# Strassen's scheme for the second product of a token mixer, with the mixer cut into thirds

## The chip, the cores and the metric

The kernel runs on one core of one Trainium2 chip. The metric is the device time of one execution in microseconds (us). Each version was run several times; quoted times are medians of the fast runs. A profile is one execution of its own, so its span differs a little from the median.

## The reference, cut to what matters

```python
# attention (recurrent, gated): B=4 batches, H=8 heads, S=768 tokens, D=48
state = f[:, :, t, :, None] * state + np.einsum('bhd,bhe->bhde', k[:, :, t], v[:, :, t])
y[:, :, t] = np.einsum('bhd,bhde->bhe', q[:, :, t], state)
# mixer, on x = y as (4, 768, 384):
xt = x.transpose(0, 2, 1)
h = xt @ U @ V                       # rank 32, over tokens
u = x + h.transpose(0, 2, 1)
ch = np.maximum(u @ w_ch1, 0.0) @ w_ch2   # 384 -> 1536 -> 384
out = u + ch
```

Everything is float32. "First product" is `u @ w_ch1`, "second product" is the one by `w_ch2`.

## The kernel before

Attention works on 16 units (a batch and a pair of heads each). Each unit is prepared on VectorE, ScalarE and GpSimd while TensorE (PE) works on an earlier one. The mixer of a batch comes as a list of pieces that are put between the attention pieces of the next batch; for the last batch nothing is left to put them between. The builder then orders each engine's instructions by itself, and each engine runs its own list in that order.

The mixer's two products, in halves of 384 tokens:

```python
def ch1(a, i):
    pm = ps_mm.tile([P, 512], F32, name="pz", tag="mm")      # ps_mm has 2 buffers
    for m in range(NDC):
        nc.tensor.matmul(pm[:, 0:HALF], lhsT=w1[:, m, i * P : (i + 1) * P], rhs=uT[a][:, m, :],
                         start=(m == 0), stop=(m == NDC - 1))
    z[a, i] = zp.tile([P, HALF], F32, name="z")
    nc.scalar.activation(z[a, i], pm[:, 0:HALF], AF.Relu)

def ch2(a, s):
    t = a * TPH + s
    pm = ps_mm.tile([P, 512], F32, name="po", tag="mm")
    for i in range(NFC):                                      # 12
        nc.tensor.matmul(pm[:, 0:DM], lhsT=z[a, i][:, s * P : (s + 1) * P], rhs=w2[:, i, :],
                         start=(i == 0), stop=(i == NFC - 1))
    o = three.tile([P, DM], F32, name="o")
    nc.vector.tensor_tensor(o, x[:, t, :], pm[:, 0:DM], ALU.add)
    nc.sync.dma_start(out=out[b, t * P : (t + 1) * P, :], in_=o)
```

The preparation of a unit in batches 2 and 3 (units 8 to 15), cut:

```python
def gates():
    fT = one.tile([P, S], F32, name="fT")                # the pool "one" has one buffer a name
    turned(fT, r["f"])                                   # VectorE, 32x32 transposes
    nc.scalar.activation(by_chunk[:, :, 1:C], fv[:, :, 1:C], AF.Sigmoid)   # into fz[n % 2]
    ...
def keep():   X = one.tile(...); nc.vector.tensor_tensor_scan(X backwards, fz, ends ...)  # shortened
def keys():   turned(kT, r["k"]); nc.gpsimd.tensor_tensor(kT, kT, X, ALU.mult)
def read():   Y = one.tile(...); nc.vector.tensor_tensor_scan(Y, fz, starts ...)          # shortened
def queries(): turned(qT, r["q"]); nc.gpsimd.tensor_tensor(qT, qT, Y, ALU.mult)
```

## Time and profile before

| | before |
|---|---|
| time, median (range of 4 runs) | 589.89 us (589.7 to 591.07) |
| PE busy / VectorE / ScalarE / GpSimd | 550.6 / 244.8 / 121.8 / 62.4 us |
| first matmul of the second product (po) | at 115.0 us |
| last stage (mixer of batch 3 alone) | from 490.2 to 583.4 us |

The engine line of the page gives busy time and share of the span. In a group's row stand the line and engine, the output tile and its inputs, the shapes and the count, then busy time and the mean of one, then the idle time just before and what ended it. The chain of waits goes back from the last instruction to whatever released each step. The prediction shows these for the kernel before.

### The profile page before, as it was taken

The numbers are of one execution on the slowest core, as the hardware profiler recorded it, in microseconds if no ns is written. First come the engines' busy times: TensorE is split into PE (matmuls) and PEld (weight loads), VectorE is DVE, ScalarE is ACT, GpSimd is POOL, SyncE is SP. The second block draws the span as 40 slices with busy tenths as digits, with TensorE's granted clock in tenths as the row PEclk, the third lists the DMA queues.
The fourth block names the chain that finished last, engine by engine and source line by source line (L and its number), as shares of the span: only waits on it lengthen the run. The fifth ranks groups of instructions, "written<-read, shape, count | busy, mean of one in ns | idle before, by whom it ended". The sixth has DMA issues, their size and how long they took to land.

```text
span 589.1 us, 8824 instructions
## 1 busy us (share of the span) xinstructions
PE 550.6 (93%) x3737; PEld 344.2 (58%) x3737; DVE 244.8 (42%) x367; ACT 121.8 (21%) x260; POOL 62.4 (11%) x59
## 2 busy tenths in 40 slices
PE   5798897799989999989969999999999999999996
PEld 4687553457656556646645556566566555555553
DVE  5768769826697340638361620254211020000000
ACT  2233346502322103210112102120022003201200
POOL 2111125500022000113020200022000000000000
PEclk9557799999999999989998999999999999999998
DMA  9699827614652135133340310010000000000000
GB/s 167 145 225 177 189 59 208 150 35 104 164 128 54 43 83 132 42 79 94 100 107 0 87 41 13 1 21 14 28 1 1 15 13 14 1 13 27 2 14 31
DMA packets 75295, 41.56 MB, mean 71 GB/s; under 512 B 65774, under 2 KB 68846, under 8 KB 75246
## 3 DMA queue, kind: packets, MB, share of 16 engines
q1 hardware_dynamic: 75246, 40.91, 29.7%
q8 instruction: 31, 0.51, 0.4%
q14 instruction: 18, 0.15, 0.1%
HBM read 36.18 MB, written 4.72 MB: 69 GB/s over the span
## 4 chain that ended last, share of the span: by engine, by line
PE 80%; DVE 11%; DMA 3%; SPq 2%; ACT 1%; issue 1%; POOL 0%; DVEq 0%; ACTq 0%; POOLq 0%
PE po L158 32%; PE pz L149 26%; PE sc L404 5%; PE y L467 4%; PE pu L133 3%; PE pt L326 3%; DVE w_y L62 2%; DMA w_raw<-in_moe_V_dram 2%; PE y L458 2%; PE ds L430 2%; PE put L142 2%; DVE w_y L63 1%; SPq L232 1%; DVE X L358 1%; DVE Y L375 1%
## 5 line engine op out<-in xcount | busy, mean ns | idle before, releaser
L149 PE MATMUL pz<-uT,w 128*128 128x384 f32 x576 | 199.2, 497 | 13.1 <-ACT z L152 12.6
L158 PE MATMUL po<-w,z 128*128 128x384 f32 x576 | 192.2, 492 | 3.7 <-ACT z L152 3.7
L149 PEld LDWEIGHTS pz<-uT,w 128*128 128x128 f32 x576 | 106.3, 191 | 85.7 <-ACT z L152 12.9
L158 PEld LDWEIGHTS po<-w,z 128*128 128x128 f32 x576 | 109.0, 191 | 80.6 <-issue 5.9
L161 DVE TENSOR_TENSOR o<-x,po 128x384 f32<-128x384 f32 x24 | 13.3, 555 | 204.7 <-PE po L158 204.7
L152 ACT ACTIVATE z<-pz 128x384 f32<-128x384 f32 x96 | 46.8, 489 | 167.0 <-PE pz L149 167.0
L410 DVE TENSOR_TENSOR A<-sc,causal 128x768 f32<-128x768 f32 x32 | 30.3, 947 | 63.2 <-PE sc L404 63.2
L358 DVE TENSOR_TENSOR_SCAN X<-fz,ends 128x768 f32<-128x768 f32 x16 | 28.1, 1755 | 33.1 <-ACT fz L347 23.9
L341 POOL TENSOR_TENSOR kT<-kT,X 128x768 f32<-128x768 f32 x8 | 14.6, 1820 | 243.4 <-DVE kT L307 243.4
L404 PE MATMUL sc<-qT,kT 48*128 48x128 f32 x384 | 38.9, 312 | 0.2 <-DVE kT L338 0.2
L404 PEld LDWEIGHTS sc<-qT,kT 48*128 48x128 f32 x384 | 29.6, 204 | 14.2 <-issue 11.2
L467 PE MATMUL y<-v_nat,A 128*64 128x48 f32 x768 | 31.0, 245 | 0.0
L64 POOL TENSOR_TENSOR w<-w_y,w_r 128x384 int32<-128x384 int32 x24 | 23.9, 995 | 65.1 <-DVE w_y L63 65.1
L375 DVE TENSOR_TENSOR_SCAN Y<-fz,starts 128x768 f32<-128x768 f32 x16 | 28.1, 1756 | 5.8 <-POOL qT L341 5.2
L467 PEld LDWEIGHTS y<-v_nat,A 128*64 128x64 f32 x768 | 28.5, 159 | 1.7 <-issue 0.3
L473 ACT COPY x<-y 128x576 f32<-128x576 f32 x16 | 10.2, 636 | 61.2 <-PE y L467 61.2
L458 PE MATMUL y<-st,qT 48*64 48x48 f32 x640 | 18.0, 242 | 5.0 <-DVE st L441 3.6
L144 ACT COPY uT<-put 128x384 f32<-128x384 f32 x24 | 10.7, 480 | 53.7 <-PE put L142 53.7
L458 PEld LDWEIGHTS y<-st,qT 48*64 48x64 f32 x640 | 13.9, 149 | 13.0 <-issue 5.0
L62 DVE TENSOR_SCALAR w_y<-w_y 128x384 uint32<-128x384 uint32 (+1 forms) x27 | 20.3, 752 | 0.7
L133 PE MATMUL pu<-h,V 128*128 128x384 f32 x48 | 19.4, 514 | 0.8 <-DVE x L134 0.8
L341 POOL TENSOR_TENSOR qT<-qT,Y 128x768 f32<-128x768 f32 x8 | 17.2, 2156 | 17.8 <-DVE X L365 11.7
(61 smaller groups left out, 338.0 us busy)
## 6 DMA issues: line engine op xcount, KB each, us to landing
w_raw<-in_moe_w_ch_dram SPq DMA_DIRECT2D x24, 384.0 KB, 3.7
v_nat<-in_v_dram SPq DMA_DIRECT2D x32, 144.0 KB, 2.8
out_dram<-o SPq DMA_DIRECT2D x24, 192.0 KB, 1.9
f_raw<-in_f_logit_dram SPq DMA_DIRECT2D x31, 142.0 KB, 3.1
k_raw<-in_k_dram SPq DMA_DIRECT2D x31, 142.0 KB, 3.4
q_raw<-in_q_dram SPq DMA_DIRECT2D x31, 142.0 KB, 3.3
f_raw<-in_f_logit_dram SPq DMA_DIRECT2D x16, 144.0 KB, 4.9
k_raw<-in_k_dram SPq DMA_DIRECT2D x16, 144.0 KB, 5.0
```

The lines of the kernel that those rows point to most:

```text
L62: nc.vector.tensor_scalar(y, y, 3, 0x3FFFFFFF, ALU.logical_shift_left, ALU.bitwise_and)
L133: nc.tensor.matmul(pm[:, 0:DM], lhsT=V[:, t * P : (t + 1) * P], rhs=h[0], start=True, stop=True)
L149: nc.tensor.matmul(pm[:, 0:HALF], lhsT=w1[:, m, i * P : (i + 1) * P], rhs=uT[a][:, m, :], start=(m == 0), stop=(m == NDC - 1))
L152: nc.scalar.activation(z[a, i], pm[:, 0:HALF], AF.Relu)
L158: nc.tensor.matmul(pm[:, 0:DM], lhsT=z[a, i][:, s * P : (s + 1) * P], rhs=w2[:, i, :], start=(i == 0), stop=(i == NFC - 1))
L341: nc.gpsimd.tensor_tensor(t, t, T[of], ALU.mult)
L358: nc.vector.tensor_tensor_scan(backwards(X, S - 1, S), backwards(f, S, S), backwards(ends, S - 1, S), 0.0, ALU.mult, ALU.add,)
L375: nc.vector.tensor_tensor_scan(Y, f[:, 0:S], starts, 0.0, ALU.mult, ALU.add)
L404: nc.tensor.matmul(sc[:, par, c * C : (c + 1) * C], lhsT=T["k"][rows[par], chunk[g * G + c]], rhs=T["q"][rows[par], chunk[g * G + c]], sta ...
L410: nc.vector.tensor_tensor(T["A"][:, :, g * G : (g + 1) * G, :], sc[:, :, 0 : G * C].rearrange("p h (c i) -> p h c i", i=C), causal.unsquee ...
L458: nc.tensor.matmul(o(a, par, c), lhsT=T["q"][rows[par], c * C + a * HC : c * C + (a + 1) * HC], rhs=T["st"][rows[par], c - 1, :], start=(c ...
L467: nc.tensor.matmul(o(a, par, c), lhsT=T["A"][:, par, c, halves[a]], rhs=vt[:, c, par, :], start=False, stop=True, skip_group_check=True,)
```

## The change

Its intent: the second product of batches 1 to 3 takes 7 products of half size in place of 8, so PE streams an eighth less there. For this the mixer works on pairs of token blocks (thirds of 256 tokens), z and w2 are added and subtracted in quarters on VectorE, and the results are put together from PSUM. To make room, the gate tile fT shares the one buffer of Y.

```diff
+        def ch1(a, j):                       # two 128-row pieces of w1, 256 tokens: one PSUM bank
+            for i in range(2):
+                for m in range(NDC):
+                    nc.tensor.matmul(pm[:, i * 2 * P : (i + 1) * 2 * P], lhsT=w1[...], rhs=uT[a][:, m, :], ...)
+            nc.scalar.activation(z[a, c][:, k : k + 2, :]..., pm, AF.Relu)
...
+        def sums_of(a):                      # VectorE, 128x768 each, in the buffers of w_raw
+            add(S[1], part(a, 1, 0), part(a, 1, 1), ALU.add)
+            add(S[2], S[1], part(a, 0, 0), ALU.subtract)
+            add(S[3], part(a, 0, 0), part(a, 1, 0), ALU.subtract)
+            add(S[4], part(a, 0, 1), S[2], ALU.subtract)
...
+        def seven(a, step):                  # step 0 of 4; the others alike, tile name pw
+            if step == 0:
+                pm = products(a, (part(a, 0, 0), w2[:, 0:NI, lo]), (S[2], sums[2]))
+                nc.scalar.copy(s[:, hi], pm[:, lo])
+                add(s[:, lo], x0[:, lo], pm[:, lo], ALU.add)
+                add(s[:, hi], s[:, hi], pm[:, hi], ALU.add)
...
+        for a in range(NA - 1):
+            ahead = first(a + 1)
+            self.main += ready(a) + ahead[: NI // 2] + second(a) + ahead[NI // 2 :]
+        self.main += ready(NA - 1)
+        self.after = second(NA - 1)
...
-            fT = one.tile([P, S], F32, name="fT")
+            fT = one.tile([P, S], F32, name="fT", tag="Y")
...
-            Y = T["Y"] = one.tile([P, S], F32, name="Y")
+            Y = T["Y"] = one.tile([P, S], F32, name="Y", tag="Y")
...
+            if b == 1:
+                after.append((1, last_sum))  # w2's upper right quarter becomes a sum, in place
```

## The prediction

> **What bounds the kernel now.** I read the page's engine line first, then the groups, the chain of waits in order of time, the timeline around the holes that the chain shows, and the windows view for the clock. The engine line and groups:
>
> ```profile
> PE 550.6 (93%) x3737; PEld 344.2 (58%) x3737; DVE 244.8 (42%) x367; ACT 121.8 (21%) x260; POOL 62.4 (11%) x59
> L149 PE MATMUL pz<-uT,w 128*128 128x384 f32 x576 | 199.2, 497 | 13.1 <-ACT z L152 12.6
> L158 PE MATMUL po<-w,z 128*128 128x384 f32 x576 | 192.2, 492 | 3.7 <-ACT z L152 3.7
> L410 DVE TENSOR_TENSOR A<-sc,causal 128x768 f32<-128x768 f32 x32 | 30.3, 947 | 63.2 <-PE sc L404 63.2
> ```
>
> PE is the bound: 93% busy, and the two mixer products are 391 of its 551 us. VectorE has 42%, and so looks like a place with room. The 497 ns of one matmul is latency; the rate is in the chain, in whose last stage nothing but PE works:
>
> ```profile
> 490.22 23.49 PE pz L149 x72
> 513.71 23.22 PE po L158 x72
> 536.92 23.22 PE pz L149 x72
> 560.14 23.23 PE po L158 x72
> ```
>
> 23.22 us by 72 is 322.5 ns for one instruction of 384 columns. Until about 113 us the start is bound by loading and converting weights on VectorE: about 1.95 us for each of the twelve pieces of w2, back to back. From 114.96 us (first po) to 583.4 us PE is the chain but for a few holes. In the starts of matmuls I find three of over 1.5 us: 1.8 us at 174, 2.0 at 255, 4.9 at 304. The timeline at the largest:
>
> ```profile
> 302.58 1.81 POOL L341 TENSOR_TENSOR qT<-qT,Y 128x768 f32<-128x768 f32 x1 [3.91 <-DVE X L365]
> 304.42 1.76 DVE L375 TENSOR_TENSOR_SCAN Y<-fz,starts 128x768 f32<-128x768 f32 x1 [1.73 <-POOL qT L341]
> 306.09 2.06 DVE L307 STREAM_TRANSPOSE fT<-f_raw 128x768 f32<-128x768 f32 x1
> 308.19 0.84 ACT L353 ACTIVATE fz<-fT 128x762 f32<-128x762 f32 x1 [6.56 <-DVE fT L307]
> 308.93 0.47 ACT L152 ACTIVATE z<-pz 128x384 f32<-128x384 f32 x1
> 309.46 3.66 PE L149 MATMUL pz<-uT,w 128*128 128x384 f32 x6 [4.71 <-ACT z L152]
> ```
>
> This is the shape of all three. The eviction of pz takes 0.47 us, but stands in ScalarE's queue behind a sigmoid that waits for VectorE's transpose of the gates, which stands behind VectorE's queue, which waits for GpSimd. Both PSUM buffers of the mixer are full meanwhile, and PE stops. It costs twice, as the windows view shows after two of the holes, where the clock is half:
>
> ```profile
> 257.80:261.20 3.40, 3.40 (x7) 1.72 (x6) 0.00 (x0) 0.00 (x0) 0.00 (x0) 0.50 0.00 0
> 309.00:312.40 3.40, 2.94 (x5) 1.73 (x6) 0.00 (x0) 1.38 (x4) 0.00 (x0) 0.50 0.00 0
> ```
>
> Each half-clock window loses 1.7 us, so the holes and their windows come to 8.7 + 3.4 = about 12 us of 468.
>
> **What the Trainium skill says.** (1) "TensorE: Matmul & The Clock Gate", section "Wait — 56ns, not 53.3ns?": a warm matmul of N columns starts every N / 2.4 GHz + about 2.5 ns. The trace agrees if an f32 instruction streams its columns twice: 768 / 2.4 + 2.5 = 322.5 ns. (2) The same page, "LDWEIGHTS (loading the stationary operand)": 128 columns take 128 / 1.2 = 107 ns whatever the moving size, and are pulled ahead. The narrowest case here, the 128x128 transposes of x, start every 109 ns with a load each, so a load also hides behind 160 ns. (3) The same page, "The two states you'll see" under Part 1: an idle window of about 3.4 us halves the clock. The trace has the 3.4 us windows at half clock. (4) "GPSIMD Engine Reference", section 8: GpSimd shares its SBUF interfaces with VectorE instructions of two SBUF inputs. The trace agrees: a 128x6 TENSOR_SCALAR with a median of 172 ns took 1.60 us beside a GpSimd multiply that itself took 3.03 us in place of 1.82.
>
> **The change, part by part.**
>
> *Second product.* Before, batches 1 to 3 have 3 x 6 blocks x 12 = 216 f32 matmuls, 432 instructions of 322.5 ns = 139.3 us. After, 9 pairs x 7 products x 6 = 378 matmuls, 756 instructions of 192 columns, each 384 / 2.4 + 2.5 = 162.5 ns, = 122.9 us. Saved: 16.4 us.
>
> *First product.* 576 x 322.5 = 185.8 us become 864 instructions of 256 columns at 215.8 ns = 186.5 us: +0.7. So PE's stream shrinks by 15.7 us; 5.3 us of that lie in the last stage, where nothing can hide it.
>
> *VectorE.* A 128x768 addition is 0.95 us (the row of A), 384 columns 0.55 us (the row of o), so 192 about 0.35. For each pair: four sums of z, 3.8 us, and evictions of 3.4 us in place of 1.1. Nine pairs: +55 us, plus four sums of w2 at about 1.35 us: VectorE goes from 245 to about 305 us. That is still no bound on average. The first w2 sum stands in VectorE's queue amid the weight conversions that set the start of po: +1.4 us on the path.
>
> *Evictions of pz.* 96 of 384 columns become 72 of 512; each PSUM buffer lasts 2.6 us of PE in place of 1.9. It is a little easier on ScalarE.
>
> *The gate tile.* fT gets the one buffer of Y. Before, VectorE turned the gates far ahead (the last fT at 306 us, while the last kT comes at 404 us). Now fT of unit n+1 must wait until GpSimd has read Y of unit n. The built order of instructions shows it: in each unit of batches 2 and 3 VectorE now runs kT, qT, (wait for GpSimd), fT, (wait for the sigmoid), X, Y in one row, 2.1 + 2.1 + 1.9 + 2.1 + 0.9 + 1.8 + 2.2 = 13 us, with the new additions ahead of it or inside, and evictions that PE needs behind it.
>
> *Walking the new order by hand* with those durations, from the last matmul that VectorE waits for, I get these PE waits: around units 8 and 9 (end of batch 1) 2.3 us on state steps behind fT, then 6.4 us, since a state product needs a PSUM buffer whose eviction is behind Y of unit 9; 1.5 us in the first transition, where the in-place sum of w2 stands ahead of the additions to x; unit 11, 4.6 us (pz eviction behind the sigmoid); unit 12, 2.2; unit 13, 1.5; unit 14, 5.8 in three parts; unit 15, 2.0. Together 26.3 us, and two or three half-clock windows, 4.3 us: 30.6 in place of 12.1 and the 0.8 of the old transition, so +17.7 us. In the last stage the sums lie under three pieces of pz (7.8 us against 3.8), except for the last pair, where about 0.3 us show.
>
> *Sum:* 589.8 - 15.7 + 1.4 + 17.7 + 0.3 = 593.5 us. A walk like this takes every alignment at its worst, as PE's delay in one place gives VectorE a lead in the next. I take off a third of the added waits: about 588 us.
>
> **Rivals.** *A: the saving goes through.* The waits stay at the 12 us of before, and the time is 589.8 - 15.7 + 1.4 = about 575.5 us. For it: VectorE has a mean of 50% and preparations run a unit ahead of their use. Against it: the holes of before come from queue order, not from load, and the new order has more behind each sigmoid. *B: VectorE's row of preparation and sums takes the saving back,* as walked: 584 to 594 us. For it: the new order on VectorE and ScalarE, and the three holes of before of exactly this kind. *C: VectorE or GpSimd become slower by sharing SBUF,* as all 36 sums of z have two SBUF inputs and GpSimd multiplies beside them: another 1 us for each of some 16 multiplies, so up to 600 us and more. For it: the 1.60 and 3.03 us above; against it: only two cases before. *D: weight loads bound the narrow matmuls.* 756 loads of 190 ns (as recorded) in place of 162.5 would give back 20 us; the 109 ns transposes speak against it. DMA is no rival: its mean share is about a third or less after 233 us.
>
> **Range and chances.** B is the likeliest, and A and B overlap around 580. I put 588 us, with 80% in 574 to 600: the low end is A with hardly any slack, the high end B in full with part of C. Faster by over 2% means under 578 us, which needs nearly all of A: 0.22. Slower by over 2% means over 601.5 us: 0.08. Within: 0.70.
>
> **What would show it.** Right: pw instructions every 162.5 ns and pz every 215.8 in the last stage, which is then about 88 us in place of 93; VectorE busy about 305 us; the first po of batch 0 about 1.4 us later; more PE idle put down to ScalarE's z, to VectorE's o or w_y, and more half-clock stretches between 170 and 400 us than two. Wrong: PE holes of no more than 12 us in all in that stretch (then A, about 575 us), or pw at 190 ns (then D), or evictions at 512 columns that hold PE in the last stage.

## More of the kernel before

One more view is needed later: who waited for whom while the weights are loaded (82 to 115 us), with total, count and longest wait:

```profile
ACT w_y L59 <- POOL w L64: 10.0, 14, 0.9
PE pz L149 <- ACT z L152: 6.3, 4, 1.8
```

In this stretch ScalarE converts weights and also evicts pz; PE stands still 6.3 us for those evictions.

## The result and the profile after

| | before | after |
|---|---|---|
| time, median | 589.89 us | 584.25 us (583.41 to 585.78, 4 runs) |
| PE / VectorE busy | 550.6 / 244.8 us | 538.2 / 301.8 us |
| first po | 115.0 us | 110.8 us |
| first po to start of last stage | 375.3 us | 377.3 us |
| last stage | 93.2 us | 88.2 us |

The ratio is 0.9903, with a 95% interval of 0.9879 to 0.9928. Ratios here are the mean time of one kernel's fast runs over the mean of the other's of the same rounds, so they are not quite ratios of the medians. The change is faster by 1%, where PE's stream alone became 2.7% shorter.

Engines and groups of the page after:

```profile
PE 538.2 (93%) x4349; PEld 443.0 (76%) x4349; DVE 301.8 (52%) x461; ACT 121.5 (21%) x245; POOL 60.7 (10%) x59
L157 PE MATMUL pz<-uT,w 128*128 128x256 f32 x864 | 196.3, 384 | 3.5 <-ACT z L162 3.1
L194 PE MATMUL pw<-w,w_raw 128*128 128x192 f32 x432 | 76.4, 329 | 2.4 <-DVE w_raw L186 1.4
L194 PE MATMUL pw<-w,z 128*128 128x192 f32 x324 | 60.8, 339 | 8.9 <-DVE w_y L210 4.5
L407 DVE STREAM_TRANSPOSE fT<-f_raw 128x768 f32<-128x768 f32 x8 | 16.7, 2084 | 11.8 <-POOL qT L441 11.8
```

VectorE is at 302 us, as worked out. The last row is new: VectorE stands still 11.8 us for GpSimd before it may turn gates. The chain in the last stage gives the rates:

```profile
488.13 23.58 PE pz L157 x108
511.71 13.65 PE pw L194 x84
525.36 15.54 PE pz L157 x72
540.90 13.65 PE pw L194 x84
```

13.65 us by 84 is 162.5 ns, and 15.54 by 72 is 215.8 ns: PE streams without a pause, weight loads hidden. So the scheme delivers 5.0 of the 5.3 us that it promises where nothing else runs. In the middle the change delivers nothing: the stretch from the first po to the last stage is 2 us longer, though by the count of matmuls 10.4 us of stream are gone from it. The timeline at the first large hole, at the end of batch 1:

```profile
178.88 1.81 POOL L441 TENSOR_TENSOR qT<-qT,Y 128x768 f32<-128x768 f32 x1 [1.95 <-DVE Y L475]
180.72 2.08 DVE L407 STREAM_TRANSPOSE fT<-f_raw 128x768 f32<-128x768 f32 x1 [1.99 <-POOL qT L441]
182.90 0.84 ACT L453 ACTIVATE fz<-fT 128x762 f32<-128x762 f32 x1 [8.89 <-DVE fT L407]
183.76 1.76 DVE L458 TENSOR_TENSOR_SCAN X<-fz,ends 128x768 f32<-128x768 f32 x1 [0.96 <-ACT fz L453]
186.06 1.76 DVE L475 TENSOR_TENSOR_SCAN Y<-fz,starts 128x768 f32<-128x768 f32 x1
187.74 0.53 DVE L174 TENSOR_TENSOR o<-x,po 128x384 f32<-128x384 f32 x1
188.37 0.79 PE L530 MATMUL ds<-v_nat,kb 128*64 128x48 f32 x20 [4.43 <-issue]
```

Each line is start, duration, engine, line, operation, tiles, and in brackets how long the engine was idle before and for whom. GpSimd reads Y until 180.7; only then may VectorE write fT into the same buffer; the sigmoid, X and Y follow one by one; and behind them stands the 0.53 us eviction `o` whose PSUM buffer PE needs for ds. The profile calls PE's 4.43 us "issue", but the state product starts just after that eviction ends. The windows view shows the price paid after such holes, or from within one (columns: stretch, length, busy time and count of PE, weight loads, VectorE, ScalarE, GpSimd, then granted clock, DMA share and GB/s):

```profile
189.20:192.60 3.40, 3.40 (x9) 2.64 (x10) 1.65 (x6) 0.00 (x0) 0.00 (x0) 0.50 0.98 265
339.40:346.20 6.80, 4.82 (x15) 4.82 (x16) 3.96 (x6) 0.58 (x2) 0.00 (x0) 0.50 0.06 24
```

10.2 us at half clock cost at most 5.1 us, where the kernel before had 6.8 us, or at most 3.4 lost; PE was busy in 8.2 of the 10.2 us, as the second stretch begins inside a hole of 4.5 us. Finally, the start. The same view of waits as before, 82 to 115 us:

```profile
ACT w_y L59 <- POOL w L64: 9.9, 13, 1.6
PE pz L157 <- ACT z L162: 2.7, 3, 1.0
```

PE waits 3.6 us less for evictions between the conversions, and the second product starts 4.1 us earlier.

### The profile page after: what moved, and what is told of

Read it like the earlier page. It is cut to its first block, busy times and chain, and to the rows that moved or that the text cites. A ratio compares the mean times of both kernels' runs of the same rounds, so it can differ in the third digit from the quotient of the medians.

```text
span 581.7 us, 10123 instructions
## 1 busy us (share of the span) xinstructions
PE 538.2 (93%) x4349; PEld 443.0 (76%) x4349; DVE 301.8 (52%) x461; ACT 121.5 (21%) x245; POOL 60.7 (10%) x59
## 4 chain that ended last, share of the span: by engine, by line
PE 65%; DVE 19%; issue 4%; DMA 3%; ACT 3%; POOL 2%; SPq 2%; DVEq 0%; ACTq 0%; POOLq 0%
PE pz L157 24%; PE pw L194 18%; PE po L171 5%; PE sc L504 4%; DVE fT L407 3%; PE y L567 3%; PE pu L138 3%; PE pt L426 3%; DVE X L458 2%; DVE qT L407 2%; DMA w_raw<-in_moe_V_dram 2%; DVE w_y L62 2%; POOL qT L441 2%; DVE Y L475 2%; PE ds L530 2%
## 5 line engine op out<-in xcount | busy, mean ns | idle before, releaser
L157 PE MATMUL pz<-uT,w 128*128 128x256 f32 x864 | 196.3, 384 | 3.5 <-ACT z L162 3.1
L157 PEld LDWEIGHTS pz<-uT,w 128*128 128x128 f32 x864 | 162.5, 191 | 28.4 <-ACT z L162 4.7
L194 PE MATMUL pw<-w,w_raw 128*128 128x192 f32 x432 | 76.4, 329 | 2.4 <-DVE w_raw L186 1.4
L162 ACT ACTIVATE z<-pz 128x512 f32<-128x512 f32 x72 | 42.8, 595 | 160.2 <-PE pz L157 156.1
L194 PEld LDWEIGHTS pw<-w,w_raw 128*128 128x128 f32 x432 | 71.2, 191 | 4.1 <-DVE w_raw L186 2.8
L194 PE MATMUL pw<-w,z 128*128 128x192 f32 x324 | 60.8, 339 | 8.9 <-DVE w_y L210 4.5
L194 PEld LDWEIGHTS pw<-w,z 128*128 128x128 f32 x324 | 54.3, 195 | 11.9 <-DVE w_y L210 5.3
L171 PE MATMUL po<-w,z 128*128 128x384 f32 x144 | 48.6, 492 | 2.4 <-ACT z L162 1.6
L171 PEld LDWEIGHTS po<-w,z 128*128 128x128 f32 x144 | 26.7, 190 | 20.9 <-issue 2.0
L573 ACT COPY x<-y 128x576 f32<-128x576 f32 x16 | 10.2, 638 | 88.3 <-PE y L567 88.3
L407 DVE STREAM_TRANSPOSE fT<-f_raw 128x768 f32<-128x768 f32 x8 | 16.7, 2084 | 11.8 <-POOL qT L441 11.8
```

Of the source, the lines that this page charges most:

```text
L157: nc.tensor.matmul(pm[:, i * 2 * P : (i + 1) * 2 * P], lhsT=w1[:, m, o : o + P], rhs=uT[a][:, m, :], start=(m == 0), stop=(m == NDC - 1))
L162: nc.scalar.activation(z[a, c][:, k : k + 2, :].rearrange("p i t -> p (i t)"), pm, AF.Relu)
L171: nc.tensor.matmul(pm[:, 0:DM], lhsT=z[a, i // NI][:, i % NI, s * P : (s + 1) * P], rhs=w2[:, i, :], start=(i == 0), stop=(i == NFC - 1))
L194: nc.tensor.matmul(pm[:, n * HM : (n + 1) * HM], lhsT=lhs[:, i, :], rhs=rhs[:, i, :], start=(i == 0), stop=(i == NI - 1))
L407: nc.vector.transpose(t.rearrange("p (i c) -> p c i", c=TB), bass.AP(src_tile.tensor, src_tile.offset, [list(src_tile.ap[0]), [D, TB], [1, ...
```

## The experiments

Two theories were open. Theory 1: the shared buffer of fT and Y takes VectorE's freedom to look ahead, and this makes the added PE waits. Theory 2: VectorE's added work makes them by itself. A third question was where the earlier start comes from. "First po", holes and half-clock stretches below are read from each run's trace. Ratios are to the kernel before in the same rounds.

| run | median us | ratio, 95% interval | result |
|---|---|---|---|
| own_fT | 574.36 | 0.9743, 0.9700 to 0.9786 | correct |
| before_shared | 592.16 | 1.0025, 0.9983 to 1.0068 | correct |
| thirds | 590.16 | 0.9989, 0.9943 to 1.0035 | correct |
| no_sums | 578.43 | 0.9796, 0.9756 to 0.9836 | wrong |
| own_no_sums | 577.75 | 0.9770, 0.9715 to 0.9825 | wrong |
| own_split0 | 574.03 | 0.9700, 0.9648 to 0.9752 | correct |
| own_s3pool | 577.02 | 0.9754, 0.9697 to 0.9811 | correct |
| fz_in_place | 576.50 | 0.9747, 0.9693 to 0.9801 | correct |
| thirds_own | 581.99 | 0.9864, 0.9826 to 0.9901 | correct |
| in_place_x2 | 579.67 | 0.9837, 0.9807 to 0.9867 | correct |
| in_place_y2 | 577.61 | 0.9796, 0.9762 to 0.9829 | correct |
| own_plain_last | 569.49 | 0.9664, 0.9628 to 0.9699 | wrong |

**own_fT: the gate tile in a buffer of its own.**

```diff
-            fT = one.tile([P, S], F32, name="fT", tag="Y")
+            fT = one.tile([P, S], F32, name="fT")
-        h[0] = two.tile([P, DM], F32, name="h", bufs=1)
+        h[0] = two.tile([P, WP], I32, name="w_r").bitcast(F32)   # to make room
```

> The changed kernel, with its gate tile fT in a buffer of its own again (the room comes from putting the small tile h into the buffers of w_r, which are idle after the weights). Theory 1, the shared buffer of fT and Y is what made the added PE waits (about 12 us beyond those of before): they mostly go, no hole over 2.5 us is left between 160 and 400 us, and the time is 573 to 577 us. Theory 2, the added VectorE work (sums and evictions, 55 us) makes the waits by itself: the holes stay within 3 us of what they were, time 581 to 585 us. If both share it: 577 to 581. Either way the last stage stays at 88 us.

574.36 us: some 10 us off the changed kernel (0.9743 against 0.9903), and the first version clear of the 2% line. This run also moved h; thirds_own and fz_in_place below gain without that move, so the gain is read as the gate tile's. The view by tile shows what came back, as min/median/max duration in ns, then the first and last start; the lines are of the kernel before, the changed one and this one:

```profile
L307 DVE STREAM_TRANSPOSE fT<-f_raw x8: 2058/2080/2121, 143.5 to 306.1; 128x768 f32<-128x768 f32 x8
```

```profile
L407 DVE STREAM_TRANSPOSE fT<-f_raw x8: 2073/2085/2093, 168.2 to 393.8; 128x768 f32<-128x768 f32 x8
```

```profile
L407 DVE STREAM_TRANSPOSE fT<-f_raw x8: 2059/2083/2127, 140.5 to 296.3; 128x768 f32<-128x768 f32 x8
```

With a buffer of its own the last gates are turned 97 us earlier than with Y's. The hole of 4.4 us before ds is gone, and the half-clock time falls from 10.2 to 3.4 us. My limit of 2.5 us for any hole was missed: waits of 3.5, 3.3 and 2.4 us remain.

**before_shared: the shared buffer alone, in the kernel before.**

```diff
-            fT = one.tile([P, S], F32, name="fT")
+            fT = one.tile([P, S], F32, name="fT", tag="Y")
-            Y = T["Y"] = one.tile([P, S], F32, name="Y")
+            Y = T["Y"] = one.tile([P, S], F32, name="Y", tag="Y")
```

> The kernel before, with nothing changed but that fT shares the one buffer of Y. Theory 1: the loss of looking ahead alone opens new PE holes at the end of batch 1 and in batches 2 and 3: 595 to 600 us against 589.9. Theory 2: without the added VectorE work the later preparation still fits, 589 to 592 us.

The ratio is 1.0025 with an interval across 1: no clear loss. The trace has a new hole of 4.2 us at 178 us, but those of before at 255 and 304 us became smaller (2.0 to 1.8 and 4.7 to 1.5). So theory 1 in its plain form fell: the shared buffer has no fixed price. That the order which the builder makes around it decides is argued, not shown.

**thirds: the mixer in thirds without Strassen's scheme, fT shared. thirds_own: the same with fT in its own buffer.**

```diff
-        return Mixer(nc, b, x_tiles[b], U, V, w1, w2, sums if b else None, ident, ...)
+        return Mixer(nc, b, x_tiles[b], U, V, w1, w2, None, ident, ...)      # and no sums of w2
```

> The changed kernel without Strassen's scheme in any batch: mixer in thirds of 256 tokens, fT still in Y's buffer, no sums. The PE stream is 16.4 us longer than in the changed kernel. The start: the first po should come near 110.8 us as in the changed kernel if the larger pz pieces (9 evictions in place of 12) brought it forward by 4 us, and near 115 or later if something else did. Theory 1 (shared buffer makes the waits): about 594 us, as waits of some 8 us come on top of 589.9 - 4.1 + 0.7. Theory 2 (VectorE's additions make them): about 586.5 us.

> Thirds of 256 tokens without Strassen's scheme, fT in its own buffer: the fourth corner beside before_shared, thirds (590.2 us) and own_fT (574.4 us). If the shared buffer costs about 10 us whatever the second product is, 580 us, and Strassen's scheme is then worth 6 us with either buffer. If the shared buffer costs little without the scheme, as in the kernel before (1.8 us), 585 to 589 us, and the scheme is worth 11 to 15 us of its 16.4 where fT has its own buffer.

These complete a square. With the shared buffer, thirds take 590.2 us and Strassen's scheme 584.3; with fT's own buffer, 582.0 and 574.4. So the buffer costs 8 us without the scheme and 10 with it, and the scheme is worth 6 us with the shared buffer and 8 with the own one (there with h moved as well), of 16.4 us of stream. The time of thirds lies between the two that I had stated for it. Neither of my two forms for the shared buffer held: it costs much in thirds, and nothing clear in halves. The first po came at 111.2 and 111.6 us, so the earlier start belongs to the thirds. And thirds with fT alone, thirds_own, beat the kernel before by 8 us, more than the whole change did.

**no_sums and own_no_sums: the sums of z left out, with shared and own buffer.** Their outputs are wrong, which doesn't matter for the times.

```diff
-            add(S[1], part(a, 1, 0), part(a, 1, 1), ALU.add)     # and S[2], S[3], S[4]
+            S[1], S[2], S[3], S[4] = part(a, 1, 0), part(a, 0, 0), part(a, 1, 0), part(a, 0, 1)
```

> The changed kernel with the four sums of z left out for each pair: the seven products read parts of z directly, so the result is wrong on purpose; PE's stream, evictions and the shared buffer of fT stay. It takes 36 VectorE instructions, at least 34 us, away. Theory 2: waits shrink by most of the added 12 us, 573 to 577 us. Theory 1: only the waits directly on sums go (some 2 to 3 us), 580 to 583 us.

> Both suspects taken away together: the gate tile in its own buffer and the four sums of z left out (wrong on purpose). Alone they took 10 and 6 us from the changed kernel. If they make the same waits (one waits for what the other queues), the two together give little more than the buffer alone: 570 to 573 us. If they make separate waits, they add: 567 to 569 us. The PE stream is that of the changed kernel, so below about 562 us (584.2 less its whole 24 us of waits) nothing is possible.

With the shared buffer, 6 us went, between my two forms: the sums share in the waits. With the own buffer, nothing went; at 0.9770 against 0.9743 it is, if anything, slower, outside what I had expected. VectorE fell from 301 to 267 us of busy time and PE still waits, for example 5.3 us at 249 us:

```profile
245.26 2.08 DVE L400 STREAM_TRANSPOSE fT<-f_raw 128x768 f32<-128x768 f32 x1
...
249.40 1.80 POOL L434 TENSOR_TENSOR qT<-qT,Y 128x768 f32<-128x768 f32 x1 [6.17 <-DVE starts L459]
251.24 1.76 DVE L468 TENSOR_TENSOR_SCAN Y<-fz,starts 128x768 f32<-128x768 f32 x1 [1.97 <-POOL qT L434]
253.09 0.84 ACT L446 ACTIVATE fz<-fT 128x762 f32<-128x762 f32 x1 [7.29 <-DVE Y L468]
253.83 1.07 ACT L162 ACTIVATE z<-pz 128x512 f32<-128x512 f32 x2
254.47 1.97 PE L187 MATMUL pw<-w,z 128*128 128x192 f32 x5 [5.33 <-ACT z L162]
```

GpSimd's multiply has waited 6.2 us for VectorE, where two transposes of 2.1 us stood in front of the small instruction that it needs (that and the second transpose are in the cut lines); then VectorE in turn waits 2.0 us for GpSimd. The sigmoid waits for VectorE's scan (the buffer that it writes is still read), and two evictions wait behind the sigmoid on ScalarE. What holds PE in this hole is the order of instructions in three queues. Theory 2, as a matter of VectorE's busy time, fell too: 34 us less of it gave nothing here. (Without the sums the products read z itself and hold it longer, but in ScalarE's list of waits none is for a buffer of z.)

**own_split0: twice as many eviction instructions in batch 0.**

```diff
+            if b: ...                                     # as before
+            else:
+                for i in range(2):
+                    nc.scalar.activation(z[a, c][:, k + i, :], pm[:, i * 2 * P : (i + 1) * 2 * P], AF.Relu)
```

> As own_fT (574.4 us, first po at 110.0 us), but in batch 0 each pz of 512 columns is evicted by two instructions of 256 columns, so 18 evictions in place of 9 stand in ScalarE's queue between the weight conversions. If the start is set by pz evictions waiting their turn in that queue, the first po moves back by 2 to 6 us, and the time with it, to 576 to 580 us. If the start moved for another reason (order of VectorE, fewer bytes), the first po stays within 0.7 us of 110.0 and the time at 574 us.

The first po stayed at 110.3 us, and the time at 574.03. So the number of eviction instructions, and their summed duration, is not what moved the start. The two halves stand side by side in ScalarE's queue, so a piece still waits one turn among the conversions. The chains of waits count these turns (see the start, in the next section); no run changed their number alone.

**own_s3pool: one of four sums on GpSimd.**

```diff
-            add(S[3], part(a, 0, 0), part(a, 1, 0), ALU.subtract)
+            nc.gpsimd.tensor_tensor(S[3], part(a, 0, 0), part(a, 1, 0), ALU.subtract)
```

> As own_fT, with one of the four sums of z (the one that depends on no other) computed by GpSimd. It takes nine instructions of about 1 us from VectorE. If VectorE's queue still makes waits: 571 to 573.5 us. If the sharing of SBUF between the two engines counts more, or GpSimd's own multiplies come later for it: 575 to 579 us.

577.02 us; the interval of its ratio overlaps that of own_fT, so no gain is seen. The remaining half-clock time grew from 3.4 to 10.2 us. Taking work from VectorE did not help here either.

**fz_in_place: no gate tile at all.**

```diff
-            fT = one.tile([P, S], F32, name="fT", tag="Y")
-            turned(fT, r["f"])
+            turned(f[:, 0:S], r["f"])
...
+            nc.vector.memset(by_chunk[:, :, 0], 0.0)
```

> The changed kernel without any gate tile: VectorE turns the gates straight into the two buffers of fz, the sigmoid works in place, and one memset of 128x6 puts the zeros back. It needs no memory, and looks ahead by up to two units, though only after the scans of the unit two earlier have read fz. If looking ahead is what counts: 573 to 577 us, as own_fT. If the private buffer gave its gain in another way: about 584 us.

576.50 us with 0.9747: the same as own_fT within the noise, by another way of looking ahead, and without memory. That supports the freedom to look ahead, rather than something about that one buffer, as what own_fT gave back.

**in_place_x2 and in_place_y2: a second buffer for X, or for Y.** Both stand on fz_in_place, with h moved as in own_fT to make room.

```diff
-            X = T["X"] = one.tile([P, S], F32, name="X")
+            X = T["X"] = one.tile([P, S], F32, name="X", bufs=2)      # in_place_y2: Y alike
```

> As fz_in_place (576.5 us), with h in the buffers of w_r and, with the room that this leaves, two buffers for X, so that VectorE's scan for the next unit no longer waits for GpSimd to read X (2.0 us at a time in own_fT's timeline). If that wait is part of what holds evictions back: 571 to 574 us. If GpSimd's wait for Y remains the longest: 575 to 577 us.

> The same with two buffers for Y in place of X: the scan Y no longer waits for GpSimd (1.7 us in own_fT's hole of 3.5 us at 275 us, 1.7 in the one of before at 304 us). If this wait sits in front of the sigmoid and the eviction: 571 to 574 us. Otherwise 575 to 577 us.

579.67 and 577.61 us: neither helps, and X with two buffers is slower than fz_in_place. The waits for GpSimd that I wanted to remove were real, but the new order put others in their place: both have 10.2 us of half clock, where fz_in_place had 6.8. More buffers are not a gain in themselves.

**own_plain_last: the last pair of batches 1 and 2 in the plain way.**

```diff
-            if sums is None:
+            if sums is None or (a == NA - 1 and b < 3):
```

> As own_fT (574.4 us), but the last pair of batches 1 and 2 is multiplied in the plain way; seven of nine pairs keep Strassen's scheme. PE's stream grows by 2 x (15.5 - 13.7) = 3.7 us. In own_fT's trace PE waits 3.3 us for a sum of z and 2.4 us for an eviction at the end of batch 1, where no pieces of pz stand between the sums and the products. If these two waits are the scheme's own cost there and go with it: 571 to 574 us. If other waits take their place, or the evictions were waited for because of VectorE's other work: 576 to 579 us.

The result is wrong, by my mistake: the change turns a quarter of w2 into a sum in place, and the plain product then reads it. The time still measures the right amount of work in the same instructions: 569.49 us, 5 us less than own_fT, although PE has 3.7 us more to stream. PE's longest waits from 110 us to the last stage, in own_fT:

```profile
PE pz L157 <- ACT z L162: 3.5, 1, 3.5
PE pw L194 <- DVE w_raw L186: 3.3, 1, 3.3
PE pw L194 <- DVE w_y L210: 2.4, 1, 2.4
PE po L171 <- ACT z L162: 1.6, 1, 1.6
```

and here:

```profile
PE pz L157 <- ACT z L162: 3.5, 1, 3.5
PE po L171 <- ACT z L162: 1.6, 1, 1.6
PE pu L138 <- DVE x L139: 0.7, 1, 0.7
```

The two waits of 3.3 and 2.4 us (for a sum of z, and for an eviction of the first part product) are gone, and nothing took their place. They stood at the end of batch 1, where no pieces of the first product lie between the sums and the products that need them. The stretch from the first po to the last stage fell from 367.9 to 363.0 us. So for these two pairs the scheme costs more in waits than it saves in stream. That explains only a part: 5.7 us less of waits and 3.7 more of stream make 2.0 of the 4.9 us, and the other 2.9 I have not assigned. A correct version would keep that sum of w2 in a buffer of its own; no run tried it, so what that version takes stays open.

## Why the prediction was right or wrong

The time was inside the range, 3.7 us below the 588 predicted, and "within 2%" was the likeliest answer and came true. Its steps fared differently.

**Readings of the kernel before.** Two were too wide. Not all three holes have the shape of the largest. At 174 us the eviction of pz stood behind a small copy on ScalarE that waited 1.9 us for VectorE's scan X. At 255 us it stood behind a sigmoid that waited for the scan Y, not for a transpose. What they share is an eviction behind a ScalarE instruction that waits for VectorE. And the TENSOR_SCALAR of 1.60 us reads one tensor, so it is no case of VectorE instructions with two SBUF inputs.

**PE's stream, -15.7 us: right.** pw runs at 162.5 ns and pz at 215.8 ns, and the last stage takes 88.2 us as stated. Rival D, the weight loads, is out: each is recorded at about 190 ns and still hides behind 162.5 ns of matmul.

**VectorE at about 305 us: right,** 301.8 measured.

**The start, "+1.4 us on the path": this step failed.** The sum of w2 did run amid the conversions, 1.35 us long at 104.3 us, and it did lengthen one of their steps in the chain, from 1.95 to 3.09 us. What I had taken as given is the number of conversions ahead. In both kernels the first po starts right after an eviction of pz that stands behind a conversion in ScalarE's queue, before the last pieces of w2 are converted. From 87 us to the first po the chain of waits passes through thirteen conversions in the kernel before and ten in the changed one (eleven in thirds, which has no sum of w2). Three steps of 1.95 less 1.14 for the sum are 4.7 us; the row begins 0.4 us later, and 4.1 were measured. PE's waits for evictions of pz fell from 6.3 to 2.7 us with it. So the traces show through which queue, and the thirds runs that it belongs to the new shape of the first product; that larger and fewer pieces wait for fewer conversions is argued, as no run changed that number alone. In numbers the term was -4.1 in place of +1.4, and this 5.5 us is more than the whole miss of 3.7.

**The middle, "+17.7 us" for a stretch that also loses 10.4 us of stream: right in kind, and right in size after the third that I took off.** These are the longest PE waits of the changed kernel from 110 to 488 us, in total, count and longest:

```profile
PE pw L194 <- DVE w_y L210: 4.5, 1, 4.5
PE ds L530 <- issue: 4.4, 1, 4.4
PE pw L194 <- ACT z L162: 4.4, 2, 2.7
PE po L171 <- ACT z L162: 1.6, 1, 1.6
```

Walked through unit by unit in the trace, the 26.3 us of predicted waits are about 18 us, so the mechanism held place by place, most of them at a smaller size: at units 8 and 9, 0.9 and 4.4 (predicted 2.3 and 6.4); 0.8 in the transition (1.5); then 2.7 (4.6), 0.5 (2.2), 0.9 (1.5), 5.9 (5.8) and 1.7 (2.0). The half-clock loss was at most 5.1 us (4.3). With the discount I expected the stretch from the first po to the last stage to grow by 17.7 x 2/3 - 10.4 = 1.4 us; it grew by 2.0. The third was a guess, and in part it was lucky: the listed waits and the half clock grew by 10.0 us, which with the stream makes -0.4. By the windows view PE's idle time in this stretch rose from 9.5 to 18.8 us, but its busy time fell by 7.2 us (365.7 to 358.5) and not by 10.4; up to 1.7 of these 3.2 us are the added half clock, the rest I have not assigned. Summed over the profiled executions: -4.1 at the start, +2.0 in the middle, -5.0 in the last stage, which is -7.1 of the 7.4 us by which the spans differ (589.1 and 581.7).

**The rivals.** B came true, at the low edge of its 584 to 594 us. own_fT comes to A's figure, 574.4 us against 575.5 stated, though by other terms: against the kernel before, its first po is 5.0 us earlier, its middle 7.4 us shorter (10.4 of stream) and its last stage 5.0. So what stood between the change and most of its saving was the gate tile's buffer. That refines my mechanism: the order that the buffer forces costs 10 us, which the walk did not separate from the sums. no_sums shows the sums to have a part with the shared buffer (6 us); own_no_sums shows none with the own one. C exists but is small. Of one line's nine additions of z, two took 2.56 us where the median is 0.95 (minimum, median and maximum in ns below), at 332.7 and 386.4 us, and both lie beside a GpSimd multiply, which itself took 2.3 us in place of 1.8; of the other 27 sums one took 2.34 us:

```profile
L187 DVE TENSOR_TENSOR w_raw<-z x9: 951/951/2564, 247.7 to 564.9; 128x768 f32<-128x768 f32 x9
```

No run tested what this costs PE.

**Where the rest of the expected gain went.** Even with fT's own buffer the scheme is worth 8 us of 16.4. By the traces of thirds_own and own_fT, the span fell by 8.5 us: 1.6 before the first po, 5.0 in the last stage, and only 1.9 in the middle, where the stream of the second product is 10.9 us shorter. Of the 9.0 us lost there, 5.7 are the waits of 3.3 and 2.4 us that own_fT shows above and thirds_own has not; they are turned into a gain by own_plain_last, though with a wrong result. The other 3.3 us I have not assigned.

**Open:** why halves do not suffer from the shared buffer as thirds do; why fewer conversions stand before the first po in thirds; some 3 us of the middle both in own_fT against thirds_own and in own_plain_last against own_fT; what a correct own_plain_last would take. The best correct versions are own_fT and own_split0, 574.4 and 574.0 us, both some 10 us below the changed kernel.

## What to carry to other kernels

A shorter stream on the bound engine paid in full only where that engine did not wait for another one's queue: the same scheme gave nearly its whole saving in the last stage and, with either buffer, little or none in the middle. Before you pay for such a change with a buffer that lets another engine work ahead, time that step alone (here it cost 8 to 10 us with thirds and nothing clear with halves), and do not read an engine's busy share as its slack: look at what stands in front of each eviction in its queue. Try the parts of a change alone, too: thirds with the gate tile's own buffer gave 8 us, more than the whole change.

## What the Trainium skill lacked or had wrong

- "TensorE: Matmul & The Clock Gate", section "Wait — 56ns, not 53.3ns?": the interval N / 2.4 + 2.5 ns is given without a word on float32, and the four passes that "FP8 and Floating Point Precision" names under "TensorE Precision Notes" come without a time. Here each float32 matmul is two instructions, and each takes its columns twice: 162.5, 215.8 and 322.5 ns for 192, 256 and 384 columns.
- The same page, "LDWEIGHTS (loading the stationary operand)": 107 ns for 128 columns, where the records show about 190 ns. Yet loads behind 162.5 ns matmuls cost nothing, so the recorded length is not the interval at which loads can follow one another, and the section does not say that the two differ.
- The same page, "The two states you'll see": an idle window of about 3.4 us is given as what halves the clock. Here a hole of 2.0 us, at 255 us in the kernel before, was followed by 3.4 us at half clock, and one of 2.7 us, at 256 us in the changed kernel, by none.
- "TensorE: Matmul & The Clock Gate", section "Architectural detail: the array is 16× 32×32, not 1× 128×128", says that ScalarE and VectorE take their queues strictly in order; no page gives the cost of an eviction that waits behind other work there: up to 5.3 us of PE for evictions of about 0.6 us, plus the half clock after it.
